# A spectral-filter and GEGLU kernel: another order in its opening, another split of its first weight loads, and its middle spectral stage two places sooner

## The chip, the cores and the metric

The kernel runs on one core of a Trainium2 chip. A core has five engines with instruction streams of their own: TensorE (PE, matrix products, written into PSUM banks), VectorE (DVE), ScalarE (ACT, table functions), GpSimd (POOL) and SyncE (SP, which here only issues DMAs). They wait for each other by semaphores; each works through its own stream in order. DMAs are issued from SP's, ScalarE's and GpSimd's queues. The metric is the device time of one execution in microseconds (us); shorter is better.

## The reference

The input x has 2048 rows of 640 numbers (bf16). What is computed:

```
xn = layernorm(x)                                  # each row: (x - mean) / sqrt(var + 1e-5)
s  = irfft2( rfft2(xn) * (w_r + 1j*w_i) )          # spectral filter over both axes
g  = silu( (gelu(xn @ w_gate) * (xn @ w_up)) @ w_down )   # 640 -> 1536 -> 640
out = x + s * g
```

## The kernel before, in words

Rows are split into 16 slabs of 128 (row index = 16 * partition + slab). `X` holds all of them. Four slabs make a group of 512 columns for the products; `xnT[g]` is the transposed, normalised group.

PE's work is one list, `back`, written out by hand. An item of it is called a place here. A second list, `plan`, says what else is emitted behind each place: `put(s, f, args)` adds a call behind place s. So the order of every engine's stream is the order of emission: first what stands outside the lists, then place 0 and what is put there, place 1, and so on. A tile framework puts in the semaphores; nothing is reordered.

- Before place 0: loads are issued; `warm_pe` runs products on a tile of ones; slab 0 is normalised (`stats`, `root_act`, `norm_parts`) and transposed on PE in two parts (`slab_Tparts`: three blocks and two blocks, through the PSUM pool `psB`, then copied out into `xnT[0]`).
- Places 0 to 15: the first group's products for hidden tiles 0 to 7 (a hidden tile is 128 of the 1536). A hidden tile takes five products with gate weights `Wg` into bank `psg`, evicted by ScalarE with Gelu into `ge` (L837), and five with up weights `Wu` into bank `psu`, evicted by VectorE, which multiplies with `ge` into `UT` (L839). Each of `psg` and `psu` has two buffers, `ge` three. Places 0 and 1 do tiles 0 and 1 for slab 0 and for slab 1 (128 columns each); places 2 to 7 tiles 2 to 7 for both slabs (256 columns); places 8 to 15 tiles 0 to 7 for slabs 2 and 3. In between slabs 1, 2 and 3 are normalised and transposed.
- Places 16 to 35: tiles 8 to 11 at 512 columns, then the down products of group 0. Places 36 to 71, 72 to 107 and 108 to 143: groups 1, 2 and 3. The down products of groups 1 and 2 (places 60 to 71 and 96 to 107) are done by a scheme with seven products in place of eight (`product`, L933).
- The spectral filter runs between these. A forward stage (`slab_S1`, `slab_D`, up to place 56) writes `ZDR` in DRAM; `load_B2` at place 56 reads it back in another order. The middle stage, 12 calls of `s2_step`, starts at place `sb` = 67: PE products `px` from the read-back tile, VectorE products with the filter, PE products `pu`, copies into `RX` and DMAs to `UDR`. `load_V` reads that back, and the inverse stage (`slab_S1i`, `slab_Di`, `group_*`, `finish`) follows at distances counted from `sb`.

A slab's statistics are two `bn_stats` and one `bn_aggr` on VectorE (`bn_half`, `bn_join`). The inverse root comes in two ways: `root_act` (ScalarE's inverse-root table) for slab 0, and `root` (a VectorE add, then a power on GpSimd) for the others. After slab 0's root ScalarE loads the Gelu table. `inv_consts` and `inv_rest` make small constants of the inverse transform on VectorE and GpSimd, at places 0 and 1; `ft_v` (ScalarE) reads them from place 8 on. `tinv_phase` and `ft_phase` (GpSimd) prepare arguments for sine tables; `root` and `shift` of slabs 4 to 7 stand behind them on GpSimd, and `norm_act` of these slabs (ScalarE, from place 15 on) reads what they make.

The lines of the loads, in order of issue on SP: L94 to L106; on ScalarE's queue L231 and L232. `load_w(k, t0, t1)` loads gate (k = 0) or up (k = 1) weights of hidden tiles t0 to t1 - 1: 640 rows of (t1 - t0) * 256 bytes.

Of the kernel before, what the change touches and what calls it, by code (L numbers as in the profile page):

```python
# [14 lines left out]
P = 128  # L15
# [61 lines left out]
def build(nc, env):  # L77
# [8 lines left out]
    def load_w(k, t0, t1, eng=nc.sync):  # L86
        f0, f1 = t0 * P, t1 * P
        eng.dma_start(out=(Wg, Wu)[k][:, :, f0:f1], in_=(wgv, wuv)[k][:, :, f0:f1])

    def load_gu(t0, t1):  # L90
        for k in range(2):
            load_w(k, t0, t1)
# [3 lines left out]
    load_w(1, 0, 2)  # L96
    load_w(1, 2, 4)
    load_x(2, 1)
    load_w(1, 4, 6)
    load_x(3, 1)  # L100
    load_gu(6, 8)
    load_x(4, 4)
    load_gu(8, 12)
    load_x(8, 4)
# [68 lines left out]
    def c1(name, dt=FP32):  # L173
        return consts.tile([P, 1], dt, name=name)
# [27 lines left out]
    def root(n0, n):  # L202
        m = mva[n0 // 4][:, n0 % 4:n0 % 4 + n, :]
        ve = work.tile([P, 4], FP32, tag="ve", name="ve")[:, 0:n]
        nc.vector.tensor_scalar(out=ve, in0=m[:, :, 1], scalar1=1e-5, scalar2=None, op0=ALU.add)  # L205
        r = work.tile([P, 4], FP32, tag="rst", bufs=4, name="rst")[:, 0:n]
        nc.gpsimd.tensor_tensor(out=r, in0=ve, in1=mhalf[:, 0:n], op=ALU.pow)  # L207
        rall[n0] = r
        for k in range(n):
            rstd[n0 + k] = r[:, k:k + 1]  # L210

    def root_act(n1):
        rstd[n1] = c1("rst0")
        nc.scalar.activation(out=rstd[n1], in_=mva[n1 // 4][:, n1 % 4, 1:2], func=ACT.Abs_reciprocal_sqrt, bias=eps)
        nc.scalar.activation(out=warm, in_=negpi, func=ACT.Gelu_apprx_tanh)

    def norm(n1, c0=0, c1_=D):
# [10 lines left out]
    eps = c1("eps")  # L228
    nc.vector.memset(eps, 1e-5)
    nc.scalar.activation(out=warm, in_=eps, func=ACT.Abs_reciprocal_sqrt)  # L230
    for t in (0, 2, 4):  # L231
        load_w(0, t, t + 2, nc.scalar)  # L232
    b_0, b_1 = c1("b_0"), c1("b_1")
    nc.vector.memset(b_0, 320.0)
    nc.vector.memset(b_1, 0.0)
# [348 lines left out]
    def warm_pe(n):  # L584
        if not warm_bank:
            warm_bank.append(bank(0))
        for _ in range(n):
            nc.tensor.matmul(warm_bank[0][:, 0:256], lhsT=ones[:, 0:P], rhs=ones, start=True, stop=True)
# [237 lines left out]
    def ffn_piece(g, t, k, c0, c1_):  # L826
        for j in range(c0 // P, c1_ // P):
            assert ("T", 4 * g + j) in done
        ps = bank(k)[:, c0:c1_]
        WT = (Wg, Wu)[k]  # L830
        for c in range(5):
            nc.tensor.matmul(ps, lhsT=WT[:, c, t * P:(t + 1) * P], rhs=xnT[g][:, c, c0:c1_],  # L832
                             start=(c == 0), stop=(c == 4))
        flush()
        if k == 0:
            ges[t] = work.tile([P, 512], BF16, tag="ge", bufs=3, name="ge")[:, c0:c1_]
            nc.scalar.activation(out=ges[t], in_=ps, func=ACT.Gelu_apprx_tanh)  # L837
        else:
            nc.vector.tensor_tensor(out=UT[:, t, c0:c1_], in0=ps, in1=ges[t], op=ALU.mult)  # L839

    def ffn_part(g, t, h):
        for k in range(2):
            ffn_piece(g, t, k, h * 256, h * 256 + 256)

    def ffn_half(g, t, k):
        ffn_piece(g, t, k, 0, 512)
# [122 lines left out]
            if t == NT - 1:  # L969
                gated(g, j, k, ph)  # L970

    def ffn_slab(j, tk):
        for t, k in tk:
            ffn_piece(0, t, k, j * P, j * P + P)

    GG, UU = ((0, 0), (1, 0)), ((0, 1), (1, 1))

    def run(*items):
        for it in items:
            it[0](*it[1:])  # L980
# [3 lines left out]
    def norm_parts(n1):  # L984
        for a, b in PARTS:
            norm(n1, a * P, b * P)

    def slab_Tparts(n1):
        if n1 == 0:
            xnT[0] = slot(0, 5, 512)  # L990
        for (a, b), ev in zip(PARTS, (nc.vector.tensor_copy, nc.scalar.copy)):
            pt = psB.tile([P, 5, P], BF16, tag="b")
            for c in range(a, b):
                nc.tensor.transpose(out=pt[:, c, :], in_=X[:, n1, c * P:(c + 1) * P], identity=ident)  # L994
            ev(out=xnT[0][:, a:b, n1 * P:n1 * P + P], in_=pt[:, a:b, :])
        done.add(("T", n1))

    NP = 8
    STR = (1, 2)
    back = [(run, (ffn_slab, 0, GG), (norm_parts, 1), (slab_Tparts, 1), (vt_iota, 1), (ffn_slab, 0, UU),  # L1000
             (inv_consts, 0), (inv_consts, 1)),
            (run, (ffn_slab, 1, GG + UU), (stats, 2), (root, 2, 1))]
    for h in range(2):
        for t in range(0 if h else 2, NP):
            back.append((ffn_part, 0, t, h))
        if h == 0:
            back[-1] = (run, (ffn_piece, 0, NP - 1, 0, 0, 256), (slab_Tparts, 3), (ffn_piece, 0, NP - 1, 1, 0, 256))
    for g in range(4):
        for t in range(NP if g == 0 else 0, NT):
            for k in range(2):  # L1010
# [10 lines left out]
    def put(s, *item):  # L1021
        plan[s].append(item)

    put(1, inv_rest)
    put(2, norm, 2)
    put(3, bn_half, 3, 0)
    put(4, bn_half, 3, 1)
    put(4, bn_join, 3)
    put(4, root, 3, 1)
    put(4, slab_T, 2, 1)  # L1030
    put(5, norm, 3)
    for g in range(5):
        put(3 + g, ft_v, g)
        put(8 + g, ft_v, 5 + g)
# [73 lines left out]
    put(z_end, load_B2)  # L1108
    for k in range(2):
        put(TURN + k, mg_turn, k)  # L1110
    sb = 67
    AT = (0, 3, 5, 7, 9, 11, 13, 15, 17, 19, 21)
    for b in range(len(BURSTS)):
        put(sb + AT[b], s2_step, b)
# [18 lines left out]
        for k in range(n):  # L1133
            put(min(d + 8 + k, LAST), finish, n0 + k)

    warm_pe(21)
    bn_half(1, 1)
    bn_join(1)
    root(1, 1)
    norm_parts(0)  # L1140
    slab_Tparts(0)
    warm_pe(2)

    put(5, phase_const)

# [35 lines left out]
```

## Time and profile before

| | us |
|---|---|
| median of 3 runs | 193.73 (193.61 to 193.73) |
| the profiled execution | 193.65 |
| its span | 191.9 |
| PE busy | 186.1 (97%) |
| VectorE busy | 150.9 (79%) |
| ScalarE busy | 131.9 (69%) |
| GpSimd busy | 53.9 (28%) |

The span is what the profiler sees from the first to the last instruction; 1.75 us of the execution lie around it. All times below are us from the span's start. In the profile's lines "PE psg L832" is an operation of line 832 that writes `psg`; "x10" is a count; "[1.54 <-POOL nmr L456]" is idle time of that engine just before, and what ended it. "SPq" and "ACTq" are instructions of the queues that issue DMAs; a row of DMA issues ends with the us from issue to landing.

### The profile page before, as it was taken

The page shows a single profiled execution, that of the slowest core. Times are in us where ns is not written, and L with a number is a line of the kernel's source. Part 1 is how long each engine was busy: PE and PEld are TensorE (multiplying, and loading weights), DVE is VectorE, ACT ScalarE, POOL GpSimd, SP SyncE. Part 2 cuts the span into 40 slices and gives each one's busy share as a digit, 9 for nine tenths or more (in the row PEclk, how much of TensorE's full clock was granted, in tenths as well). Part 3 has the DMA queues.
Part 4 walks back from the last instruction along what each step waited for, and adds up shares of the span by engine and source line. Part 5 has one row for each costly group of instructions (what it writes and reads, how often), then busy time and mean ns, then how long its engine had stood idle before and what let it go on. Part 6 is the DMA issues. An engine that isn't in the chain of part 4 may idle for free.

```text
span 191.9 us, 4068 instructions
## 1 busy us (share of the span) xinstructions
PE 186.1 (97%) x1453; PEld 115.6 (60%) x1469; DVE 150.9 (79%) x364; ACT 131.9 (69%) x241; POOL 53.9 (28%) x91
## 2 busy tenths in 40 slices
PE   7999999999999999999999999999999999999993
PEld 5788854677655665566543334347775555556772
DVE  6787889899799889846978677685445898888973
ACT  4658557957878778536697878634989776876622
POOL 4458768999040200000000000002030134150400
PEclk9999999999999999999999999999999999999999
DMA  6999999948889994249996444149900084778842
GB/s 164 300 329 360 370 332 170 172 99 318 178 165 191 211 300 120 78 111 230 223 108 123 106 103 103 42 107 273 266 5 0 0 117 111 152 153 213 121 174 62
DMA packets 39700, 32.43 MB, mean 169 GB/s; under 512 B 12928, under 2 KB 37760, under 8 KB 39552
## 3 DMA queue, kind: packets, MB, share of 16 engines
q1 hardware_dynamic: 35888, 27.91, 58.6%
q0 software_dynamic: 1824, 3.28, 9.4%
q10 hardware_dynamic: 1968, 0.98, 1.9%
q8 instruction: 11, 0.18, 0.4%
q14 instruction: 9, 0.07, 0.1%
HBM read 19.03 MB, written 7.88 MB: 140 GB/s over the span
## 4 chain that ended last, share of the span: by engine, by line
PE 95%; DMA 2%; DVE 1%; issue 1%; SPq 0%; ACT 0%
PE psu L832 27%; PE psg L832 27%; PE psg L967 7%; PE psg L933 7%; PE psu L967 6%; PE psu L933 5%; PE pu L657 2%; PE pd L762 2%; PE pv L735 2%; PE pz L555 2%; PE pd L573 2%; PE px L628 2%; DMA X<-in_A_x_dram 2%; PE pt L994 1%; PE pd L575 1%
## 5 line engine op out<-in xcount | busy, mean ns | idle before, releaser
L832 PE MATMUL psu<-XG,Wu 128*128 128x512 bf16 (+2 forms) x284 | 60.4, 342 | 0.5 <-issue 0.3
L832 PE MATMUL psg<-XG,Wg 128*128 128x512 bf16 (+2 forms) x280 | 60.1, 341 | 0.6
L839 DVE TENSOR_TENSOR UT<-psu,ge 128x512 bf16<-128x512 f32 (+2 forms) x58 | 34.4, 594 | 13.6 <-PE psu L832 8.1
L837 ACT ACTIVATE ge<-psg 128x512 bf16<-128x512 f32 (+2 forms) x58 | 30.3, 523 | 21.3 <-PE psg L832 20.6
L832 PEld LDWEIGHTS <-Wu 128*128 128x128 bf16 x290 | 25.9, 98 | 20.9 <-issue 3.4
L832 PEld LDWEIGHTS <-Wg 128*128 128x128 bf16 x290 | 26.5, 98 | 18.8 <-issue 0.2
L967 PEld LDWEIGHTS <-UT 128*128 128x128 bf16 x204 | 19.1, 98 | 6.9
L813 POOL DMA_DIRECT2D VY<-in_A_x_dram x12 | 10.6, 964 | 26.2 <-ACT W L737 10.5
L713 POOL COPY vr<-VY 128x128 bf16<-128x128 bf16 x2 | 0.6, 291 | 60.2 <-DMA VY<-UDR 60.2
L644 DVE TENSOR_TENSOR RZ<-xs,W 128x960 bf16<-128x960 bf16 (+2 forms) x22 | 13.3, 647 | 4.4 <-ACT xs L640 4.4
L967 PE MATMUL psg<-Wd,UT 128*128 128x320 bf16 (+1 forms) x108 | 15.7, 290 | 0.0
L578 ACT CAST RZ<-pd 128x660 bf16<-128x660 f32 x16 | 11.3, 706 | 5.2 <-PE pd L575 5.2
L189 DVE BATCH_NORM_STATS2 st<-X 128x6 f32<-128x320 bf16 x32 | 14.0, 476 | 0.6 <-DMA X<-in_A_x_dram 0.4
L933 PEld LDWEIGHTS <-UT 128*128 128x128 bf16 x120 | 11.4, 98 | 4.8 <-issue 0.4
L967 PE MATMUL psu<-Wd,UT 128*128 128x320 bf16 (+1 forms) x96 | 13.9, 293 | 0.0
L737 ACT CAST W<-pv 128x640 bf16<-128x640 f32 x16 | 11.1, 691 | 3.1 <-PE pv L735 3.1
L763 ACT ACTIVATE W<-pd 128x640 bf16<-128x640 f32 x16 | 11.3, 706 | 1.5 <-PE pd L762 1.5
L557 ACT CAST GEN<-pz 128x640 bf16<-128x640 f32 x16 | 11.2, 698 | 1.2 <-PE pz L555 1.2
L672 ACT CAST RX<-pu 128x480 bf16<-128x480 f32 (+3 forms) x22 | 10.8, 489 | 1.1 <-DVE RX L672 0.3
L640 ACT CAST xs<-px 128x960 bf16<-128x960 f32 (+2 forms) x11 | 10.3, 933 | 0.0
L207 POOL TENSOR_TENSOR rst<-ve,mhalf 128x1 f32<-128x1 f32 (+1 forms) x6 | 5.5, 913 | 11.5 <-DVE ve L205 11.5
L933 PE MATMUL psg<-X,UT 128*128 128x320 bf16 x48 | 7.8, 300 | 0.0
(202 smaller groups left out, 302.1 us busy)
## 6 DMA issues: line engine op xcount, KB each, us to landing
ZDR<-RZ SPq DMA_DIRECT2D x16, 160.5 KB, 4.1
UDR<-RX SPq DMA_DIRECT2D x10, 240.8 KB, 3.1
B<-ZDR SPq DMA_DIRECT2D x8, 240.8 KB, 5.2
W<-UDR SPq DMA_DIRECT2D x2, 963.0 KB, 9.1
X<-in_A_x_dram SPq DMA_DIRECT2D x3, 640.0 KB, 10.3
Wd<-in_B_w_down_dram SPq DMA_DIRECT2D x1, 1920.0 KB, 14.6
VY<-in_A_x_dram POOLq DMA_DIRECT2D x12, 160.0 KB, 4.3
out_dram<-VY SPq DMA_DIRECT2D x12, 160.0 KB, 2.8
```

What stands on the lines that cost most here:

```text
L189: nc.vector.bn_stats(out=st_n[n1][:, k, :], in_=X[:, n1, 320 * k:320 * k + 320])
L557: nc.scalar.copy(out=Zt[n1], in_=pz)
L578: nc.scalar.copy(out=zd.rearrange("p c (q e) -> p c q e", e=10), in_=pd[:, :, 0:330].rearrange("p c (e q) -> p c q e", q=33))
L644: nc.vector.tensor_tensor(out=pp[-1], in0=xs, in1=WT[:, :, h0:h0 + n, l0:l0 + w], op=ALU.mult)
L672: copy(out=out, in_=src)
L737: nc.scalar.copy(out=vs, in_=pv)
L763: nc.scalar.activation(out=parts(eobuf, i, 5)[:, :, n1 - DG[i][0], :], in_=pd, func=ACT.Copy, scale=(2.0 if n1 // 4 in BY_SILU else 1.0) / ...
L832: nc.tensor.matmul(ps, lhsT=WT[:, c, t * P:(t + 1) * P], rhs=xnT[g][:, c, c0:c1_], start=(c == 0), stop=(c == 4))
L837: nc.scalar.activation(out=ges[t], in_=ps, func=ACT.Gelu_apprx_tanh)
L839: nc.vector.tensor_tensor(out=UT[:, t, c0:c1_], in0=ps, in1=ges[t], op=ALU.mult)
L933: nc.tensor.matmul(ps, lhsT=lhs[:, t, :], rhs=rhs[:, t, :], start=(t == 0 and i in (0, 1, 3)), stop=(t == 5), skip_group_check=i in (2, 4, ...
L967: nc.tensor.matmul(ph, lhsT=UT[:, t, j * P:(j + 1) * P], rhs=Wd[:, t, c0:c1_], start=(t == 0), stop=(t == NT - 1))
```

## The change

Six things are changed.

- Loads: ScalarE's queue issues one load, gates of tiles 0 to 3, where it issued three (tiles 0 and 1, 2 and 3, 4 and 5). SP loads gates of tiles 4 to 7 in one and up weights of tiles 4 to 7 in one.
- Order ahead of place 0: 19 warming products, then slab 0 is normalised and transposed, then 4 more; only then come the second half of slab 1's statistics and its root, which is now taken on ScalarE; the Gelu table is loaded behind it (`gelu_table`), and slab 1 is normalised.
- Places 0 to 15 are cut in another way, by a new function `ffn_multi`: several hidden tiles side by side in one bank, evicted by one instruction of 512 columns. Places 0 to 3 do tiles 0 to 3 for slab 0 (gates, ups) and for slab 1; places 4 to 7 tiles 4 to 7 for both; places 8 to 15 pairs of tiles for slabs 2 and 3. Slab transposes stand in the middle of places 1, 6 and 7.
- In `slab_Tparts` both parts of slabs 0 and 1 are copied out by VectorE.
- What is put behind places 1 to 5 for slabs 2 and 3 moves; `inv_consts` and `inv_rest` move from places 0 and 1 to place 7, ahead of `tinv_phase`.
- `sb` is 65 in place of 67: the middle stage, and with it all that is counted from it, stands two places sooner.

```diff
--- before.py
+++ after.py
@@ -96,9 +96,9 @@
     load_w(1, 0, 2)
     load_w(1, 2, 4)
     load_x(2, 1)
-    load_w(1, 4, 6)
+    load_w(0, 4, 8)
     load_x(3, 1)
-    load_gu(6, 8)
+    load_w(1, 4, 8)
     load_x(4, 4)
     load_gu(8, 12)
     load_x(8, 4)
@@ -210,8 +210,10 @@
             rstd[n0 + k] = r[:, k:k + 1]
 
     def root_act(n1):
-        rstd[n1] = c1("rst0")
+        rstd[n1] = c1("rst%d" % n1)
         nc.scalar.activation(out=rstd[n1], in_=mva[n1 // 4][:, n1 % 4, 1:2], func=ACT.Abs_reciprocal_sqrt, bias=eps)
+
+    def gelu_table():
         nc.scalar.activation(out=warm, in_=negpi, func=ACT.Gelu_apprx_tanh)
 
     def norm(n1, c0=0, c1_=D):
@@ -228,8 +230,7 @@
     eps = c1("eps")
     nc.vector.memset(eps, 1e-5)
     nc.scalar.activation(out=warm, in_=eps, func=ACT.Abs_reciprocal_sqrt)
-    for t in (0, 2, 4):
-        load_w(0, t, t + 2, nc.scalar)
+    load_w(0, 0, 4, nc.scalar)
     b_0, b_1 = c1("b_0"), c1("b_1")
     nc.vector.memset(b_0, 320.0)
     nc.vector.memset(b_1, 0.0)
@@ -838,9 +839,27 @@
         else:
             nc.vector.tensor_tensor(out=UT[:, t, c0:c1_], in0=ps, in1=ges[t], op=ALU.mult)
 
-    def ffn_part(g, t, h):
-        for k in range(2):
-            ffn_piece(g, t, k, h * 256, h * 256 + 256)
+    def ffn_multi(k, t0, n, c0, c1_, half=None):
+        w = c1_ - c0
+        for j in range(c0 // P, c1_ // P):
+            assert ("T", j) in done
+        if half in (None, 0):
+            cur["m"] = bank(k)[:, 0:n * w].rearrange("p (t w) -> p t w", w=w)
+        ps = cur["m"]
+        WT = (Wg, Wu)[k]
+        for i in range(n) if half is None else range(half * n // 2, (half + 1) * n // 2):
+            for c in range(5):
+                nc.tensor.matmul(ps[:, i, :], lhsT=WT[:, c, (t0 + i) * P:(t0 + i + 1) * P], rhs=xnT[0][:, c, c0:c1_],
+                                 start=(c == 0), stop=(c == 4))
+        if half == 0:
+            return
+        flush()
+        if k == 0:
+            ge = work.tile([P, 512], BF16, tag="ge", bufs=3, name="ge")[:, 0:n * w].rearrange("p (t w) -> p t w", w=w)
+            ges[t0, c0] = ge
+            nc.scalar.activation(out=ge, in_=ps, func=ACT.Gelu_apprx_tanh)
+        else:
+            nc.vector.tensor_tensor(out=UT[:, t0:t0 + n, c0:c1_], in0=ps, in1=ges[t0, c0], op=ALU.mult)
 
     def ffn_half(g, t, k):
         ffn_piece(g, t, k, 0, 512)
@@ -969,12 +988,6 @@
             if t == NT - 1:
                 gated(g, j, k, ph)
 
-    def ffn_slab(j, tk):
-        for t, k in tk:
-            ffn_piece(0, t, k, j * P, j * P + P)
-
-    GG, UU = ((0, 0), (1, 0)), ((0, 1), (1, 1))
-
     def run(*items):
         for it in items:
             it[0](*it[1:])
@@ -988,7 +1001,7 @@
     def slab_Tparts(n1):
         if n1 == 0:
             xnT[0] = slot(0, 5, 512)
-        for (a, b), ev in zip(PARTS, (nc.vector.tensor_copy, nc.scalar.copy)):
+        for (a, b), ev in zip(PARTS, (nc.vector.tensor_copy, nc.scalar.copy if n1 > 1 else nc.vector.tensor_copy)):
             pt = psB.tile([P, 5, P], BF16, tag="b")
             for c in range(a, b):
                 nc.tensor.transpose(out=pt[:, c, :], in_=X[:, n1, c * P:(c + 1) * P], identity=ident)
@@ -997,14 +1010,14 @@
 
     NP = 8
     STR = (1, 2)
-    back = [(run, (ffn_slab, 0, GG), (norm_parts, 1), (slab_Tparts, 1), (vt_iota, 1), (ffn_slab, 0, UU),
-             (inv_consts, 0), (inv_consts, 1)),
-            (run, (ffn_slab, 1, GG + UU), (stats, 2), (root, 2, 1))]
-    for h in range(2):
-        for t in range(0 if h else 2, NP):
-            back.append((ffn_part, 0, t, h))
-        if h == 0:
-            back[-1] = (run, (ffn_piece, 0, NP - 1, 0, 0, 256), (slab_Tparts, 3), (ffn_piece, 0, NP - 1, 1, 0, 256))
+    back = [(run, (ffn_multi, 0, 0, 4, 0, P), (vt_iota, 1)),
+            (run, (ffn_multi, 1, 0, 4, 0, P, 0), (slab_Tparts, 1), (ffn_multi, 1, 0, 4, 0, P, 1)),
+            (run, (ffn_multi, 0, 0, 4, P, 256)),
+            (run, (ffn_multi, 1, 0, 4, P, 256))]
+    for h, k, t0 in ((0, 0, 4), (0, 0, 6), (0, 1, 4), (0, 1, 6)) + tuple((1, k, t) for t in (0, 2, 4, 6) for k in range(2)):
+        back.append((ffn_multi, k, t0, 2, 256 * h, 256 * h + 256))
+    back[6] = (run, (ffn_multi, 1, 4, 2, 0, 256, 0), (slab_T, 2, 1), (ffn_multi, 1, 4, 2, 0, 256, 1))
+    back[7] = (run, (ffn_multi, 1, 6, 2, 0, 256, 0), (slab_Tparts, 3), (ffn_multi, 1, 6, 2, 0, 256, 1))
     for g in range(4):
         for t in range(NP if g == 0 else 0, NT):
             for k in range(2):
@@ -1021,14 +1034,17 @@
     def put(s, *item):
         plan[s].append(item)
 
-    put(1, inv_rest)
-    put(2, norm, 2)
-    put(3, bn_half, 3, 0)
-    put(4, bn_half, 3, 1)
-    put(4, bn_join, 3)
-    put(4, root, 3, 1)
-    put(4, slab_T, 2, 1)
-    put(5, norm, 3)
+    put(1, stats, 2)
+    put(1, root, 2, 1)
+    put(2, bn_half, 3, 0)
+    put(2, bn_half, 3, 1)
+    put(3, norm, 2)
+    put(3, bn_join, 3)
+    put(3, root, 3, 1)
+    put(5, norm_parts, 3)
+    for part in range(2):
+        put(7, inv_consts, part)
+    put(7, inv_rest)
     for g in range(5):
         put(3 + g, ft_v, g)
         put(8 + g, ft_v, 5 + g)
@@ -1108,7 +1124,7 @@
     put(z_end, load_B2)
     for k in range(2):
         put(TURN + k, mg_turn, k)
-    sb = 67
+    sb = 65
     AT = (0, 3, 5, 7, 9, 11, 13, 15, 17, 19, 21)
     for b in range(len(BURSTS)):
         put(sb + AT[b], s2_step, b)
@@ -1133,13 +1149,15 @@
         for k in range(n):
             put(min(d + 8 + k, LAST), finish, n0 + k)
 
-    warm_pe(21)
+    warm_pe(19)
+    norm_parts(0)
+    slab_Tparts(0)
+    warm_pe(4)
     bn_half(1, 1)
     bn_join(1)
-    root(1, 1)
-    norm_parts(0)
-    slab_Tparts(0)
-    warm_pe(2)
+    root_act(1)
+    gelu_table()
+    norm_parts(1)
 
     put(5, phase_const)
```

## The prediction

> **What bounds the kernel now.** I read the page first, then the chain of work that ended last in order of time, then the timeline and the DMA issues of the first 9 us, and at last the timeline of every engine from 11 to 36 us.
>
> ```profile
> span 191.9 us, 4068 instructions
> ...
> POOL 4458768999040200000000000002030134150400
> ...
> PE 95%; DMA 2%; DVE 1%; issue 1%; SPq 0%; ACT 0%
> ```
>
> The last line is the chain, by engine; the one above it is GpSimd (POOL) in 40 slices of 4.8 us, busy tenths. TensorE (PE) is the bound from the first product to the last one. Everything else can only matter by letting PE begin sooner or by making it wait. The chain shows how it begins (start, length, what):
>
> ```profile
> 1.17 3.19 DMA X<-in_A_x_dram
> 4.38 0.90 DVE st L189 x2
> ...
> 5.55 0.15 DVE ve L205
> ...
> 6.05 0.54 PE pt L994 x5
> 6.59 0.22 PE psg L588 x2
> 6.84 0.76 PE psg L832 x10
> 7.60 0.28 PE pt L994 x5
> 7.88 0.56 PE psu L832 x10
> ...
> 9.56 0.55 PE psg L832 x5
> ```
>
> The second slab's load lands at 4.36, its statistics and root run on VectorE, and only then is slab 0 normalised, though slab 0's own root was ready earlier:
>
> ```profile
> 1.18 4.55 PE L588 MATMUL psg<-GEN 128*128 128x256 bf16 x21 [1.18 <-DVE eps L229]
> ...
> 4.29 0.29 ACT L214 ACTIVATE rst<-mva,eps 128x1 f32<-128x1 f32 x1 [2.08 <-DVE mva L195]
> 4.60 1.28 ACT L215 ACT_TABLE_LOAD   x1
> ...
> 5.62 0.63 DVE L218 TENSOR_SCALAR X<-X,mva,rst 128x384 bf16<-128x384 bf16 x2
> ```
>
> **The change, part by part.** Profiled execution: 193.65 us; the median of the runs shown, 193.73, stands 0.08 above it, so I add 0.08 at the end.
>
> *Order on VectorE.* Of what stood before slab 0's normalisation, one statistics half (0.45 of the 0.90 pair) stays; the other half, the join and the root's first step move behind it. Normalisation starts at about 4.38 + 0.45 = 4.85 where it started at 5.62, 0.77 sooner. Transposes and evictions follow by the same distance, so the first product could start at 6.84 - 0.77 = 6.07. Nineteen instead of 21 warming products end at 1.18 + 19 x 0.217 = 5.30, with the transposes due at 5.28. Four instead of two behind them add 2 x 0.11: 6.29. The second eviction of slab 0 and of slab 1 moves from ScalarE to VectorE; VectorE has it done before the fourth product of a piece reads it. This part by itself is worth -0.55.
>
> *Products.* Per column block the same columns are multiplied, but tiles 2 and 3 of slabs 0 and 1 go as 40 products of 128 columns (0.56 for 10) where 20 of 256 stood (0.55 for 5): 2.24 against 2.18, +0.06. Evictions become fewer and wider on engines that PE does not wait for here: nothing.
>
> *Loads.* ScalarE's queue issues one load of 640 KB, gates of tiles 0 to 3, where it issued three of 320 KB; SP issues 14 where it issued 15, with 1 KB rows for tiles 4 to 7. What the first product waits for changes from 320 KB to 640 KB.
>
> ```profile
> 1.19 1.01 ACTq L88 DMA_DIRECT2D Wg<-in_B_w_gate_dram  x2
> 1.64 1.00 SPq L88 DMA_DIRECT2D Wu<-in_B_w_up_dram  x2
> Wg<-in_B_w_gate_dram ACTq DMA_DIRECT2D x1, 320.0 KB, 4.3
> Wu<-in_B_w_up_dram SPq DMA_DIRECT2D x1, 320.0 KB, 5.4
> Wg<-in_B_w_gate_dram ACTq DMA_DIRECT2D x1, 320.0 KB, 6.1
> Wu<-in_B_w_up_dram SPq DMA_DIRECT2D x1, 320.0 KB, 6.7
> 4.00:5.00 1.00, 1.00 (x7) 0.67 (x6) 0.84 (x4) 0.69 (x2) 0.00 (x0) 1.00 1.15 342
> 6.00:9.00 3.00, 2.92 (x45) 2.65 (x46) 2.24 (x13) 1.64 (x6) 1.17 (x2) 1.00 1.15 304
> ```
>
> The last number of an issue row is us from issue to landing, and of a window row GB/s. So the first 320 KB of gates landed at 1.19 + 4.3 = 5.5 and the second at about 1.7 + 6.1 = 7.8; the up weights at 7.05 and at 2.15 + 6.7 = 8.85. How soon 640 KB in one load lands, no row shows. If its second half comes alone, 5.5 + 320/342 = 6.45. If as many bytes of up weights come between, 5.5 + 640/304 = 7.6. I take 6.8: nearer to alone, since the gates' rows become twice as long as those of the up weights, but not alone, since the second half came 2.3 us behind the first before. PE then waits from 6.29 and starts at 6.83: -0.01 in place of -0.55, ends -0.35 and +0.8.
>
> The Trainium skill, "DMA: Bandwidth & Descriptors", section "Queues, rings and completion order", says that each DMA engine goes round robin over the queues it has work for, a packet at a time; with a row as the packet that would put half as many bytes of up weights between, and by it the gates would land at 5.5 + 480/342 = 6.9. The late landing of the second gate load agrees with it.
>
> The second half of the up weights is wanted after 1.12 + 0.56 + 0.28 = 1.96 us of products, so at 8.8, against its 8.85 of before with the same bytes ahead of it. Cost about nothing; but it caps the gain: a start at 6.29 would want it at 8.25.
>
> *Root of slab 1 on ScalarE, its table load behind it.* POOL's power and its vector step go; 0.29 on ScalarE and the 1.28 table load come at about 7.1. The first gate eviction waits for it, until about 9; its bank is wanted again by the fourth gate piece, at 6.83 + 4.76 = 11.6. Slab 1 is normalised by 7.1 + 0.29 + 0.63 = 8.0, its transposes due at 6.83 + 1.68 = 8.5. Covered; without cover the table load would cost up to 1.3.
>
> *Slabs 2 and 3.* Statistics and roots move between the pieces; by the lengths above slab 2 is normalised around 13.4 and its transposes are due at 14.3. Covered.
>
> *The inverse constants go from places 0 and 1 to place 7.* This is the part that I believe costs. POOL works in order, and the place is ahead of Tinv's phase:
>
> ```profile
> 11.84 0.26 POOL L323 TENSOR_SCALAR y_e<-pb,x_e 128x1 f32<-128x1 f32 x1
> ...
> 13.57 0.26 POOL L323 TENSOR_SCALAR k_m<-pb,y_m 128x1 f32<-128x1 f32 x1
> 15.50 2.38 POOL L334 TENSOR_SCALAR GEN<-GEN,u,ph_t 128x1024 int32<-128x1024 int32 x2 [0.67 <-DVE ph_t L282]
> 21.21 1.49 POOL L374 TENSOR_TENSOR GEN<-GEN 128x660 f32<-128x660 f32 x1
> 25.27 1.04 POOL L207 TENSOR_TENSOR rst<-ve,mhalf 128x4 f32<-128x4 f32 x1 [2.57 <-DVE ve L205]
> 26.58 0.20 POOL L456 TENSOR_TENSOR nmr<-nm,rst 128x4 f32<-128x4 f32 x1
> 26.81 0.92 ACT L461 ACTIVATE X<-X,nmr,rst 128x640 bf16<-128x640 bf16 x1 [1.54 <-POOL nmr L456]
> 27.64 0.58 ACT L837 ACTIVATE ge<-psg 128x512 bf16<-128x512 f32 x1
> 28.24 0.69 DVE L839 TENSOR_TENSOR UT<-psu,ge 128x512 bf16<-128x512 f32 x1 [0.62 <-ACT ge L837]
> 30.88 0.64 DVE L839 TENSOR_TENSOR UT<-psu,ge 128x512 bf16<-128x512 f32 x1
> 29.55 1.24 PE L832 MATMUL psg<-XG,Wg 128*128 128x512 bf16 x5
> 32.79 1.24 PE L832 MATMUL psu<-XG,Wu 128*128 128x512 bf16 x5
> ```
>
> Place 7 ends on PE 1.12 + 1.40 + 1.12 + 1.12 + 1.09 + 1.09 + 1.37 + 1.37 = 9.68 us after the start, at 16.5; its multiplication on VectorE ends near 17.4, the constants follow, and POOL's six steps (11.84 to 13.83 before) run from 17.55 to 19.5. Tinv's phase starts at 19.5 in place of 15.5. From there to the end of the third FT step POOL needs 22.70 - 15.50 = 7.2: it is free at 26.7, where the root of slabs 4 to 7 began at 25.27 after 2.57 idle. So the idle time takes most of the delay and 1.43 is left. ScalarE already waits 1.54 for nmr; it now gets it at 28.2, and its eviction of the ninth tile's gates (27.64 + 0.58) ends at 29.65. PE wants that bank at 29.55: 0.1. VectorE's multiplication behind it comes 1.45 later, the next one ends near 33.0 behind two statistics, and PE wants its bank at 32.79 + 0.1: 0.15. Together +0.27; ends 0 (if POOL's steps run shorter) and 0.7 (half of the 1.43, if VectorE's and ScalarE's lateness reaches the folds behind).
>
> *Middle stage at place 65 in place of 67* (place k is the k-th piece of PE's work). Steps, the loads that read them back and the inverse stage all come two places sooner, the distances stay. What is new is how near the first step comes to its read of ZDR:
>
> ```profile
> 82.94 6.26 SPq L603 DMA_DIRECT2D B<-ZDR  x10
> B<-ZDR SPq DMA_DIRECT2D x1, 240.8 KB, 4.1
> 88.04 1.63 PE psg L933 x12
> 89.67 0.32 PE px L628 x2
> ```
>
> The first step needs the first two of ten loads; the second is issued at about 83.55 and lands 4.1 later, at 87.65. Two products sooner than 89.67 (1.63) is 88.04. It fits by 0.4. The transposes on SP and the UDR writes keep their order. The end hangs on the last products, not on this stage. Zero; if the load were 1 us late, +0.6.
>
> *Sum:* -0.01 + 0.06 + 0.27 + 0 = +0.32; 193.65 + 0.32 + 0.08 = 194.05.
>
> **Rivals.**
> 1. *The loads come early and POOL's lateness is absorbed.* For it: the window rate of 342 before the short rows begin. Gates at 6.45, start 6.5, -0.34 + 0.06: 193.45. Against it: the cap of the up weights. To be faster by more than 0.39 it needs a start under 6.4 and no wait later: 193.3.
> 2. *The gates land late (slower).* The two queues share by bytes: 7.6, start 7.65, +0.81 + 0.06 + 0.27: 194.85. It decides from a landing of 6.9 on, with the POOL wait. For it: 2.3 us between the two gate loads of before. Against it: the short rows of the up weights.
> 3. *POOL's lateness reaches further.* The start as forecast, but the bank waits sum to 0.7: 194.5. For it: in its slices POOL stands at 8 and 9 tenths from 29 to 48 us, so nothing is made up there. Against it: from 48 us on it is idle, and most of what it makes is used later.
> 4. *PE's clock rises later.* The 21 warming products took 0.217 each, the two behind the transposes 0.11. With 19 and a pause the rise could miss its time; every us at half speed costs 0.5, so 195 with 2 us more. Against it: a pause of 0.3 stood there before too. The Trainium skill, "TensorE: Matmul & The Clock Gate", section "Part 1", has the gate open after a window of about 3.4 us of activity, and 19 products are 4.1 us; by that rule it opens in time.
> 5. *The reorder does nothing*, start and waits cancelling: 193.75.
>
> **How the numbers follow.** Forecast (193.9 to 194.2) 0.32; rival 1 0.17, of it 0.09 under 193.34; rival 5 0.13; rival 2 0.18; rival 3 0.15; rival 4 0.05. About 0.2% (0.39) is what can be told from no change: 193.34 to 194.12 holds two thirds of the forecast (0.21), 0.08 of rival 1 and rival 5, so 0.43 with rounding; slower is the rest of the forecast, 2, 3 and 4: 0.48; faster 0.09. The range goes from rival 1, 193.5, to rival 2, 194.85; the likeliest alone has 193.9 to 194.2.
>
> **What would show it.** Transposes of slab 0 near 5.3; a wait of PE before the first product released by the load of Wg, 0.3 to 0.8; Tinv's phase at 19.5; ScalarE's wait for nmr about 3 us; short waits of PE for banks at 29 to 33 us; px near 88 without a wait. Wrong would make it: a first product under 6.4 or over 7.2, or PE without any pause between 25 and 36.

## The result and the profile after

| | before | after |
|---|---|---|
| median of 16 executions each, same chip | 193.82 us | 194.77 us |
| ratio after/before, 95% interval | | 1.0053 (1.0038 to 1.0068) |
| the profiled execution | 193.65 | 194.63 |
| its span | 191.9 | 192.6 |
| time outside the span, mean | 1.78 (of the executions beside the experiments) | 1.98 |

One of the 16 executions before took 327.87 us; the ratio is taken without it. The change costs about 0.95 us. The forecast was +0.32, so the sign and the range held and the size did not. The profiled pair differs by 0.98, and its traces show where it went. First the page of the changed kernel: GpSimd's slices and the chain by engine.

```profile
span 192.6 us, 4074 instructions
...
POOL 4323999899240200000000000002110506224000
...
PE 86%; POOL 6%; DMA 3%; issue 1%; DVE 1%; SPq 1%; ACT 0%; ACTq 0%; DVEq 0%
```

GpSimd, which was on no stretch of the chain before (PE had 95%), now carries 6% of it. The chain in order of time shows it, in two windows (start, length, what):

```profile
2.10 6.13 DMA Wu<-in_B_w_up_dram
...
8.28 0.73 PE psu L852 x10
```

```profile
15.63 0.56 PE psu L852 x5
16.28 0.69 DVE UT L862
...
19.18 2.39 POOL GEN L335 x2
...
22.37 2.99 POOL GEN L373
...
25.43 1.81 POOL GEN L375
...
28.51 0.21 POOL nmr L457
...
29.57 0.58 ACT ge L838
30.20 1.24 PE psg L833 x5
```

The opening now hangs on the second load of up weights, not on the gates. From place 7 the chain goes over VectorE's multiplication, all of GpSimd's work on Tinv and FT (the tables that `tinv_phase` and `ft_phase` prepare; L335, L373 and L375), the root of slabs 4 to 7 with their shift `nmr`, and ScalarE's Gelu, and comes back to PE at 30.20. The row of the gates' load among the DMA issues, and the timelines of PE, GpSimd, ScalarE and VectorE at the same places:

```profile
Wg<-in_B_w_gate_dram ACTq DMA_DIRECT2D x1, 640.0 KB, 4.8
```

```profile
5.20 0.54 PE L1007 MATMUL pt<-ident,X 128*128 128x128 bf16 x5
5.58 0.60 PE L589 MATMUL psg<-GEN 128*128 128x256 bf16 x4
6.08 1.31 PE L852 MATMUL psg<-XG,Wg 128*128 128x128 bf16 x20
...
24.74 1.24 PE L833 MATMUL psg<-XG,Wg 128*128 128x512 bf16 x4
...
27.98 1.24 PE L833 MATMUL psu<-XG,Wu 128*128 128x512 bf16 x5
30.20 1.24 PE L833 MATMUL psg<-XG,Wg 128*128 128x512 bf16 x5 [0.97 <-ACT ge L838]
...
34.59 1.66 PE L986 MATMUL psg<-Wd,UT 128*128 128x320 bf16 x11
...
188.47 0.83 PE L986 MATMUL psg<-Wd,UT 128*128 128x128 bf16 x12
```

```profile
22.37 2.98 POOL L373 TENSOR_SCALAR GEN<-GEN 128x660 f32<-128x660 f32 x1
...
28.74 0.92 ACT L462 ACTIVATE X<-X,nmr,rst 128x640 bf16<-128x640 bf16 x1 [4.29 <-POOL nmr L457]
...
22.29 0.76 DVE L340 TENSOR_SCALAR GEN<-GEN,andm,orm 128x1024 int32<-128x1024 int32 x1
...
24.72 0.65 DVE L205 TENSOR_SCALAR ve<-mva 128x4 f32<-128x4 f32 x1
```

The matching rows of before: the first of GpSimd's two FT steps, place 16 (at 25.24), the first down products and the last products.

```profile
18.68 2.45 POOL L372 TENSOR_SCALAR GEN<-GEN 128x660 f32<-128x660 f32 x1
...
25.24 1.24 PE L832 MATMUL psg<-XG,Wg 128*128 128x512 bf16 x4
...
33.87 1.79 PE L967 MATMUL psg<-Wd,UT 128*128 128x320 bf16 x12
...
187.82 0.83 PE L967 MATMUL psg<-Wd,UT 128*128 128x128 bf16 x12
```

Read by stages, after minus before:
- First product 6.08 against 6.84: -0.76. At place 16 it is 24.74 against 25.24: -0.50. Of the gain, 0.23 went into the wait for the up weights at 8.28, and 0.06 into the 128-column products.
- From place 16 to the first down product 9.85 (34.59 - 24.74) against 8.63 (33.87 - 25.24): +1.22. It is the wait of 0.97 and what is lost around it.
- From there to the last products 153.88 against 153.95: -0.07.
- From the last products to the end of the span (the traces have it to hundredths) 192.65 - 188.47 = 4.18 against 191.87 - 187.82 = 4.05: +0.13. Part 6 shows what stands there.
- The time outside the span is 194.63 - 192.65 = 1.98 against 193.65 - 191.87 = 1.78: +0.20.

-0.50 + 1.22 - 0.07 + 0.13 + 0.20 = +0.98.

### The profile page after: what moved, and what is told of

Read it like the earlier page. It is cut to its first block, busy times and chain, and to the rows that moved or that the text cites. A ratio compares the mean times of both kernels' runs of the same rounds, so it can differ in the third digit from the quotient of the medians.

```text
span 192.6 us, 4074 instructions
## 1 busy us (share of the span) xinstructions
PE 186.0 (97%) x1473; PEld 116.1 (60%) x1489; DVE 151.2 (78%) x358; ACT 130.3 (68%) x230; POOL 53.4 (28%) x90
## 4 chain that ended last, share of the span: by engine, by line
PE 86%; POOL 6%; DMA 3%; issue 1%; DVE 1%; SPq 1%; ACT 0%; ACTq 0%; DVEq 0%
PE psu L833 21%; PE psg L833 21%; PE psg L986 7%; PE psg L952 7%; PE psu L986 6%; PE psu L952 5%; DMA Wu<-in_B_w_up_dram 3%; PE pu L658 2%; PE pv L736 2%; PE pd L763 2%; PE pz L556 2%; PE psu L852 2%; PE pd L574 2%; PE px L629 2%; PE psg L852 2%; POOL GEN L373 2%
## 5 line engine op out<-in xcount | busy, mean ns | idle before, releaser
L833 PE MATMUL psg<-XG,Wg 128*128 128x512 bf16 x190 | 48.7, 379 | 1.5 <-ACT ge L838 1.0
L833 PE MATMUL psu<-XG,Wu 128*128 128x512 bf16 x194 | 49.0, 379 | 0.5 <-issue 0.3
L840 DVE TENSOR_TENSOR UT<-psu,ge 128x512 bf16<-128x512 f32 x40 | 27.4, 687 | 12.4 <-PE psu L833 6.8
L838 ACT ACTIVATE ge<-psg 128x512 bf16<-128x512 f32 x40 | 23.9, 598 | 15.4 <-PE psg L833 14.5
L833 PEld LDWEIGHTS <-Wu 128*128 128x128 bf16 x200 | 18.0, 98 | 20.3 <-issue 3.4
L833 PEld LDWEIGHTS <-Wg 128*128 128x128 bf16 x200 | 18.6, 98 | 19.2 <-issue 1.3
L852 PE MATMUL psu<-XG,Wu 128*128 128x256 bf16 (+1 forms) x100 | 10.4, 251 | 0.1
L852 PE MATMUL psg<-XG,Wg 128*128 128x256 bf16 (+1 forms) x100 | 10.0, 251 | 0.0
```

Of the source, the lines that this page charges most:

```text
L852: nc.tensor.matmul(ps[:, i, :], lhsT=WT[:, c, (t0 + i) * P:(t0 + i + 1) * P], rhs=xnT[0][:, c, c0:c1_], start=(c == 0), stop=(c == 4))
```

## The experiments

Theory A: GpSimd's order costs the time. The constants behind place 7 delay Tinv, FT, the root and so the Gelu whose bank PE wants. Theory F, formed when the first four runs came back with unequal times outside the span: the ends of the instruction streams cost too. Rivals stand with each run. The kernel before ran beside each group: 193.72 us (first four runs), 193.57 (next four), 193.56 and 193.57.

### 1. The constants alone, taken out and put in

Inverse constants back to the middle of place 1 in the changed kernel:

```
-             (run, (ffn_multi, 1, 0, 4, 0, P, 0), (slab_Tparts, 1), (ffn_multi, 1, 0, 4, 0, P, 1)),
+             (run, (ffn_multi, 1, 0, 4, 0, P, 0), (slab_Tparts, 1), (inv_consts, 0), (inv_consts, 1), (inv_rest,),
+              (ffn_multi, 1, 0, 4, 0, P, 1)),
...
-    for part in range(2):
-        put(7, inv_consts, part)
-    put(7, inv_rest)
```

> The changed kernel with one thing undone: the inverse constants (five steps on VectorE, six on GpSimd) stand in the middle of place 1 again, ahead of Tinv's phase, instead of at place 7. Theory A (GpSimd's order costs the time): Tinv's phase starts near 14.6 instead of 19.2, the last FT step ends near 22 instead of 27.2, nmr is there near 26.3, TensorE's one wait of 1.0 us for the Gelu eviction (ended 30.20) is gone, and the time falls by 0.9 to 1.1 to 193.6 to 193.9; against the kernel before the ratio is 0.998 to 1.000. Rival B (the loss lies in the new cut of places 0 to 15, in its 512-column evictions and its bank order): the wait stays in another form and the time falls by less than 0.3, to 194.5 or more.

Measured: 194.29 us, ratio 1.003 (1.0013 to 1.0046), profiled span 191.9. Of the three rows below the first is GpSimd's, the second VectorE's and the third PE's; no wait is left near 30.

```profile
14.79 2.38 POOL L335 TENSOR_SCALAR GEN<-GEN,u,ph_t 128x1024 int32<-128x1024 int32 x2 [0.85 <-DVE ph_t L283]
...
15.44 0.69 DVE L862 TENSOR_TENSOR UT<-psu,ge 128x512 bf16<-128x512 f32 x1 [0.76 <-ACT XG L548]
...
16.45 1.25 PE L852 MATMUL psg<-XG,Wg 128*128 128x256 bf16 x10 [0.16 <-DVE XG L1008]
```

A holds for the wait: from place 16 to the first down product it is 33.81 - 25.18 = 8.63 again, to the hundredth what the kernel before takes. In the whole only half of the loss came back (0.5% to 0.3%, with intervals that overlap), less than expected. Two things took the rest. Place 8 began at 16.45 instead of 16.01: 0.1 of it came from the opening, and 0.3 because VectorE's multiplication of place 6, due at about 15.0, began at 15.44, with GpSimd's Tinv phase running beside it since 14.79. (The row names ScalarE's copy L548 as what ended the wait; in the changed kernel the same multiplication began at 14.91, before that copy had ended, so it doesn't hang on it.) And this execution took 2.17 outside its span; the twelve had 1.8 to 3.4.

The same part alone in the kernel before (constants out of place 0, `put(7, inv_consts, ...)`, `put(7, inv_rest)`):

> The kernel before with this one part of the change alone: inverse constants at place 7. Theory A: GpSimd's six steps run near 17.4 to 19.4, Tinv's phase starts there, the FT steps end near 26.7 to 27.4, nmr comes at 28.0 to 28.7, and TensorE waits 0.2 to 0.8 for the Gelu eviction of the ninth tile, near 29.6 to 30.2; less than in the changed kernel, since TensorE reaches that place 0.5 later here. Time 194.0 to 194.6, ratio 1.001 to 1.004. The prediction's term for it was 0.27, with ends 0 and 0.7. Rival B: no wait, ratio 0.999 to 1.001.

Measured: 194.36 us, ratio 1.0029 (1.0015 to 1.0044), 1.79 outside the span. GpSimd, VectorE and PE:

```profile
24.95 1.50 POOL L374 TENSOR_TENSOR GEN<-GEN 128x660 f32<-128x660 f32 x1
...
25.12 1.36 DVE L205 TENSOR_SCALAR ve<-mva 128x4 f32<-128x4 f32 x1
...
26.86 1.24 PE L832 MATMUL psu<-XG,Wu 128*128 128x512 bf16 x5 [0.52 <-DVE UT L839]
```

The part costs 0.64 by itself (from place 16 to the first down product 34.41 - 25.09 = 9.32, +0.69), but in another place than expected: not over `nmr` and the Gelu. VectorE's step `ve` on four columns (0.17 in the kernel before) took 1.36: it ended at 26.48, with GpSimd's step at 26.45. The multiplication queued behind it came late, and PE waited for its bank. The Trainium skill, "SBUF — State Buffer", section "SBUF: two separate sides", calls the port pair that VectorE and GpSimd share an exclusive lock: a GpSimd instruction or a VectorE instruction of certain forms, whichever starts first, gets it for the whole instruction, and the other is blocked. These two rows agree; rows of parts 2 and 5 do not.

### 2. Why GpSimd's two FT steps were longer

`put(14, tinv_mask, 1)` becomes `put(19, tinv_mask, 1)`:

> The changed kernel with VectorE's second mask step of Tinv (128x1024 int32) at place 19 instead of 14, so that it doesn't run beside GpSimd's FT steps. Theory C (the two FT steps of 2.98 and 1.81, which took 2.45 and 1.49 before, are held up by VectorE's mask and root step beside them): they go back to about 2.45 and 1.49, nmr comes 0.7 to 0.85 sooner, near 27.9, TensorE's wait falls from 0.97 to 0.1 to 0.4, time 193.9 to 194.2. Rival D (they are longer for another cause, the loads or ScalarE's work beside them): their lengths stay, the wait stays near 1.0, time 194.6 to 194.9.

Measured: 195.19 us (194.63 to 195.77, 6 executions), ratio 1.0076 (1.0053 to 1.0099), profiled span 192.6. GpSimd, then VectorE, then the waits of PE:

```profile
22.39 2.45 POOL L373 TENSOR_SCALAR GEN<-GEN 128x660 f32<-128x660 f32 x1
24.93 1.49 POOL L375 TENSOR_TENSOR GEN<-GEN 128x660 f32<-128x660 f32 x1
...
22.35 1.34 DVE L340 TENSOR_SCALAR GEN<-GEN,andm,orm 128x1024 int32<-128x1024 int32 x1
```

```profile
PE psg L986 <- DVE UT L840: 0.3, 1, 0.3
PE psg L833 <- ACT ge L838: 0.2, 1, 0.2
```

The steps went back to 2.45 and 1.49 and the wait near 30 to 0.24, as C says. The edit explains only the second step. Beside the first one VectorE's first mask, not moved, took 1.34 in place of 0.76: this time VectorE lost. In both traces the mask had begun first, by 0.08 in the changed kernel and by 0.04 here; in the traces of parts 3 and 4 that have the same pair it began 0.05 ahead, and GpSimd lost (3.00). So C holds, the two engines delay each other, but what decides who loses stays open. The mask ended at 23.69 while GpSimd's step ran on to 24.84, so it was held for only a part of that step. The time did not fall. The moved mask ran at 32.70, the multiplications behind it came no sooner than in the changed kernel (34.65 against 34.61), and PE waited at 36.0: the first down products began 0.68 sooner than in the changed kernel (33.91 against 34.59), the second ones only 0.07 (36.15 against 36.22). Why the executions of this run spread over 1.1 us stays open.

### 3. The loads of the opening

The changed kernel with the gates of tiles 0 to 3 in two loads:

```
-    load_w(0, 0, 4, nc.scalar)
+    load_w(0, 0, 2, nc.scalar)
+    load_w(0, 2, 4, nc.scalar)
```

> The changed kernel with the gates of the first four tiles as two loads of 320 KB (rows of 512 bytes, as in the kernel before) on ScalarE's queue in place of one of 640 KB. Theory H (the gates come early because their rows are 1 KB against 512 bytes of the up weights in the other queue, so the queues share in proportion to the row): the second gate load lands at 7.0 to 7.8 instead of 6.0, TensorE stops 0.3 to 1.0 in the middle of place 0, and the second up load lands sooner than 8.2, at about 7.5. Rival I (the 640 KB came early because one issue was saved on the queue): it lands within 0.3 of 6.0 and nothing else moves. The end comes by the wait of 1.0 near 30 either way, up to 0.4 later by theory H.

Measured: 195.51 us, ratio 1.0088 (1.0064 to 1.0113), profiled span 193.5. PE's waits:

```profile
PE psg L853 <- DMA Wg<-in_B_w_gate_dram: 1.2, 1, 1.2
PE psg L834 <- ACT ge L839: 1.0, 1, 1.0
```

H holds in its direction: with rows of 512 bytes the second half came at 7.8 (PE began with it at 7.87), with rows of 1 KB all of it at 6.0. The second up load did not come sooner, as H had it, but later (6.6 us to land against 6.1). The second row shows that PE came to place 20 about 1 us later and still waited 1.0: GpSimd's chain starts from place 7 and so moves with PE. A late opening doesn't hide it.

### 4. The ends of the instruction streams

The changed kernel with 13 one-column memsets on VectorE and 12 one-column copies on ScalarE added:

```
+    for k in range(13):
+        put(104 + 2 * k, pad_v)
+    for k in range(12):
+        put(13 if k < 4 else 14, pad_s)
```

> The changed kernel with 13 more one-column memsets on VectorE (late, from place 104 on) and 12 more one-column copies on ScalarE (places 13 and 14, where it stood idle), which compute nothing that is used. Theory F (the change took 13 recorded instructions from VectorE and 19 from ScalarE, and so the last fetch of an 8 KB block of code of each engine, which before ran at 176.4 and 186.6 inside the span, now falls at 194.0 and 194.4, behind its end, and lengthens the execution there): both fetches move back inside the span, none is left behind 192.6, the time outside the span falls from 1.9 to 2.0 to 1.75, and the execution gets 0.2 to 0.3 shorter, 194.4 to 194.6. Rival G (the fetches are idle reading and cost nothing): the time outside the span stays at 1.9 to 2.0 and the time at 194.7 to 194.9, or more by the added work.

Measured: 194.49 us, ratio 1.0045 (1.003 to 1.0059); 1.85 outside the span on the mean (median 1.81). The DMA view of 193 to 195 us, behind the span's end, of the changed kernel and of this one:

```profile
DMA packets 2, 0.02 MB, mean 8 GB/s; under 512 B 0, under 2 KB 0, under 8 KB 0
...
q14 instruction: 2, 0.02, 2.3%
```

```profile
DMA packets 0, 0.00 MB, mean 0 GB/s; under 512 B 0, under 2 KB 0, under 8 KB 0
```

F holds for the fetches and for the time outside the span, 0.13 less on the mean. The gain in the whole (1.0053 to 1.0045) has its sign, but the intervals overlap. With fewer instructions on VectorE and ScalarE the fetch of the last 8 KB of code of each fell behind the program's work. In the traces the time outside the span goes with it: 1.78 to 1.79 in six without such a fetch, 1.98 to 2.18 in five with two. But it isn't the only cause: the two traces of the kernel with place 67 in part 6 have 2.05 and 1.91 and no fetch behind the end.

The middle stage back at place 67 in the changed kernel (`sb = 67`):

> The changed kernel with the middle stage back at place 67. All theories but one: within 0.1 us of the changed kernel, since px did not wait there; the wait at 30.20 stays at 1.0 and px starts about 1.6 later. Rival E (the middle stage two places sooner costs or wins time at its end): the time moves by 0.3 or more.

Measured: 195.71 us, ratio 1.0102 (1.0081 to 1.0122). The profiled span is 192.7, as in the changed kernel, but 2.56 us lie outside it on the mean and 3.57 in the profiled execution. The same view from 193 to 197 us:

```profile
q8 instruction: 1, 0.02, 2.5%
```

A 16 KB fetch now stands there as well, taken for one of PE's code (this queue fetches 16 KB each 11 to 22 us through the kernel, one fetch for 250 to 270 of PE's recorded instructions). On PE's own path the "within 0.1" held: from place 16 to the last products 188.47 - 24.67 = 163.80 against 163.73. The loss in the whole lies mostly outside the span, by a mechanism that none of the theories had.

### 5. A version that keeps the gain

Constants ahead of place 0, where VectorE waits for ScalarE's root and GpSimd is idle:

```
     root_act(1)
     gelu_table()
+    inv_consts(0)
+    inv_consts(1)
+    inv_rest()
```

> The changed kernel with the inverse constants ahead of place 0, between the join of slab 1's statistics and its normalisation, where VectorE waits 0.37 for ScalarE's root and GpSimd is idle. Theory A: Tinv's phase starts near 14.6, nmr is there by 26.9, no wait near 30, and, other than with the constants in the middle of place 1, nothing in the opening comes later: place 16 starts at 24.7 to 24.9 against 25.24 in the kernel before, the down products at 33.3 to 33.5 against 33.87. Span 0.3 to 0.5 shorter than before; with a time outside the span of 1.9 to 2.2 the execution comes to 193.4 to 193.8. Rival: the gain of the opening isn't kept, time 194.0 to 194.4.

Measured: 193.97 us, ratio 1.0017 (0.9999 to 1.0036), profiled span 191.8, no wait near 30; but place 8 at 16.43 and place 16 at 25.16, as with the constants in place 1. The rival had it: the gain of the opening isn't kept.

With the small instructions of part 4 added:

> Both: constants ahead of place 0 and the added small instructions on VectorE and ScalarE. Theories A and F together: no wait near 30, no code fetch behind the span's end, 1.75 outside the span, time 193.2 to 193.5, faster than the kernel before by 0.2 to 0.5 (ratio 0.9975 to 0.999). If F is wrong: as the kernel without the added instructions, 193.4 to 193.8.

Measured: 193.73 us, ratio 1.0011 (0.9992 to 1.0031), 1.80 outside the span on the mean against 1.98: the same sign again, 0.24 less with 25 more instructions, within the intervals. It is no faster than the kernel before.

With `phase_const` put behind place 7 instead of place 5, so that Tinv's phase doesn't start beside place 6's multiplication:

> Constants ahead of place 0 and the added small instructions, and one thing more: the one-column VectorE step that makes ph_t, on which GpSimd's Tinv phase waits, stands behind place 7 instead of place 5, so that the phase (1.2 us a step) does not start at 14.79 beside VectorE's multiplication of place 6. Theory J (that multiplication began 0.41 late, at 15.42 to 15.48 in three runs against 14.91 in the changed kernel, because GpSimd's step had begun at 14.79; the copy of slab 3 behind it came later by as much, and place 8 with it): Tinv's phase starts near 17.0, the multiplication at 14.9 to 15.1, place 8 at 16.0 to 16.1 instead of 16.43 to 16.49, place 16 at 24.7 to 24.9, no wait near 30 (FT steps end near 24.2, nmr 26.3 to 26.6), down products at 33.35 to 33.5, span 191.3 to 191.6, time 193.1 to 193.4, ratio 0.997 to 0.999. Rival K (the delay has another cause): place 8 stays at 16.4, time 193.6 to 193.9.

Measured: **193.25 us**, ratio to the kernel before 0.9987 (0.9974 to 0.9999), where the changed kernel had 1.0053. PE and GpSimd:

```profile
16.01 1.25 PE L852 MATMUL psg<-XG,Wg 128*128 128x256 bf16 x10
...
24.75 1.24 PE L833 MATMUL psg<-XG,Wg 128*128 128x512 bf16 x4
...
17.15 2.39 POOL L335 TENSOR_SCALAR GEN<-GEN,u,ph_t 128x1024 int32<-128x1024 int32 x2 [3.22 <-DVE ph_t L283]
```

Theory J holds: place 8 is at 16.01 again, though the phase now runs later. The multiplication of place 6 began at 14.91, the down products at 33.38. What holds VectorE back for 0.41 in the first part of GpSimd's step, and not for the whole of it, stays open; the lock as the Trainium skill tells it would have held it to 15.98. This kernel is faster than the changed one by 0.66% and than the kernel before by 0.13%, with an interval just clear of 1. Its step from the version ahead of it (1.0011 to 0.9987) has the expected sign, but those two intervals still overlap.

### 6. What the two places are worth

The fastest kernel with the middle stage at place 67, twice:

> The same with the middle stage back at place 67, so that the two stand side by side without a code fetch behind the end. If the place of the middle stage is worth nothing, as the prediction's term for it says: equal within 0.15, 1.75 to 1.85 outside the span. If the 0.9 that the changed kernel lost with place 67 came from the stage itself and not from the code fetches behind the end: 0.5 to 0.9 slower.

> A second look at the fastest kernel with the middle stage at place 67, to see which of the two waits of its first profile belong to that place: the 0.75 for the gate load in the opening should be gone or small if it was the chance of one execution, and the wait of 0.5 for the read-back should be there again, 0 to 0.6, with less than 0.5 between GpSimd's copies and the product. Time 193.4 to 194.5 against 193.25 for place 65.

Measured: 194.4 us (ratio 1.0045, 1.0026 to 1.0064) and 194.65 (1.005, 1.003 to 1.0071), so by the ratios 1.1 and 1.2 us more than at place 65. PE's waits of the first and of the second, and GpSimd's copy and PE's product of the first:

```profile
PE psg L852 <- DMA Wg<-in_B_w_gate_dram: 0.8, 1, 0.8
PE pv L736 <- POOL vr L716: 0.5, 1, 0.5
```

```profile
PE psg L852 <- DVE x_w L273: 0.4, 1, 0.4
PE pv L736 <- POOL vr L716: 0.3, 1, 0.3
```

```profile
133.50 0.28 POOL L716 COPY vr<-VY 128x128 bf16<-128x128 bf16 x1
...
133.84 0.23 PE L736 MATMUL pv<-Tinv,vr 128*128 128x128 bf16 x1 [0.47 <-POOL vr L716]
```

With this earlier opening and place 67 PE waits for the read-back of the middle stage. In the kernel before the same copy ended about 0.4 ahead of its product; at place 65 it is more:

```profile
132.66 0.29 POOL L715 COPY vr<-VY 128x128 bf16<-128x128 bf16 x1
...
133.35 0.22 PE L735 MATMUL pv<-Tinv,vr 128*128 128x128 bf16 x1
```

```profile
130.84 0.36 POOL L716 COPY vr<-VY 128x128 bf16<-128x128 bf16 x1
...
132.37 0.22 PE L736 MATMUL pv<-Tinv,vr 128*128 128x128 bf16 x1
```

These are the kernel before and the changed one: 133.35 - 132.95 = 0.4 and 132.37 - 131.20 = 1.2. The two places are a cover. The other wait, for the gate load, is in both traces of this kernel (the load took 5.4 and 6.0 us to land; the second row names VectorE's `x_w`, long done, but 1.19 + 6.0 is 7.2, when PE began). The eight other traces with this load have 4.6 to 4.9. Nothing links it to the middle stage. From place 16 to the last products these two traces took 163.2 and 163.1 us, against 162.5 at place 65: 0.6 to 0.7 lies behind the opening, and the waits show 0.3 to 0.5 of it. The opening took 0.3 and 0.9 more, and the time outside the span, expected at 1.75 to 1.85, was 2.01 and 2.15 on the mean against 1.86. So the 1.1 to 1.2 isn't all the stage's.

The stage at place 65 alone in the kernel before:

> The kernel before with the middle stage at place 65 alone. Theory L (at place 67 the read-back of the middle stage's result comes only 0.4 ahead of the products that need it, and late executions wait there; two places sooner make it 1.2 or more): as the kernel before or slightly faster, ratio 0.997 to 1.000, GpSimd's copies of the read-back end 1.2 or more ahead of the product that reads them, and the slower executions get rarer. If the stage's place is worth 0.9 to 1.1 by itself, as the two pairs of the changed kernels had it: 192.5 to 192.9. If it is worth nothing, as the prediction's term says: within 0.1.

Measured: 193.91 us, ratio 1.0018 (1.0008 to 1.0029): none of the three expectations holds. The copy comes 0.7 ahead of its product (130.99 against 131.66), not 1.2, PE's last products come as early as before (187.76 against 187.82), and yet the span ends 0.3 later, at 192.2. In the trace's semaphore records, SP ends the program by waiting for its DMAs' semaphores in a fixed order, 0.06 apart. In the kernel before the last output's semaphore is the last of them. Here it is the second of nine, and the seven behind it take 0.43 more. The loss is at the program's end, not in the stage. In the changed kernel it is the seventh of nine, and the two behind it take 0.12: that is the +0.13 of its last 4 us, since the last output lands 3.05 us behind the first of the last products in both kernels.

## Why the prediction was right, and where not

- **Direction and range: right, with the mechanism named.** It gave 0.48 to slower, put the cost into the constants at place 7, and drew its path: GpSimd, nmr, ScalarE's eviction, PE's bank. The trace has this path, and moving the constants away removes the wait. That the total fell into the range is luck in part: its upper end, 194.85, was worked out from gates that land late, and they landed early.
- **"Together +0.27": mis-sized.** It measured +1.22, beyond its upper end of 0.7 (0.64 alone in the kernel before). The path's pieces: Tinv's phase at 19.18 (forecast 19.5); from there to nmr 9.5 us (28.72) against 8.7, since the two FT steps took 0.85 longer; then 1.43 through ScalarE, 1.45 in the forecast. And PE wanted the bank at 29.06, not 29.55: a place 0.5 sooner is a wait 0.5 longer where the other end is fixed by GpSimd. The step took the durations of GpSimd's instructions as fixed, when they depend on what VectorE starts beside them. Rival 3 came nearest (waits of 0.7), with a chance of 0.15.
- **"Worth -0.55" for the order on VectorE: more, -0.76 at the first product.** The transposes came at 5.20, near the forecast 5.28. The sum charged 0.22 for the two more warming products behind them; these ran from 5.58, while the copies into `xnT` were made, and the first product still began at 6.08.
- **"I take 6.8" for the gates: wrong, below both ends.** They landed at 1.19 + 4.8 (the row of the DMA issues after) = 6.0. Both ends set out from the first half's landing at 5.5. As one load with rows of 1 KB the first half must have been in by about 5.0 (an estimate: the second half at the 332 GB/s that moved from 5 to 6 us takes 1.0); as a load of its own with rows of 512 bytes it came at 5.3 in part 3. The Trainium skill's turn by packets gave 6.9, with a row taken as the packet; its direction agrees with the split loads, its time does not. In two traces of ten it was 6.6 and 7.2, on both sides of the value taken.
- **Second up weights, "caps the gain": right.** 0.23 of wait at 8.28 against a want at 8.04.
- **Products +0.06, slabs 2 and 3, root of slab 1: right.** 40 products took 11.09 - 8.85 = 2.24, and no wait stands there.
- **Middle stage "zero": right in this change** (-0.07, px at 88.69 without a wait), but short of what it does: it takes the read-back from 0.4 to 1.2 of slack, and without it the earlier PE of part 6 waits 0.3 to 0.5.
- **Clock: rival 4 is real, and small.** In the changed kernel the granted clock rose at 5.39, and the four products behind the transposes took 0.60. In the version of part 1 it rose at 6.29, they took 0.87, and the first product came at 6.45. That 19 products open the clock in time doesn't hold in general: in six of the fourteen traces it rose only at 5.99 to 7.16.
- **Missing from the sum:** the end. +0.20 of the 0.98 lies outside the span and +0.13 in the wait for the DMAs' semaphores; every line of the sum had counted both as nothing. Added instructions took 0.13 of the first back, on the mean.

Of the signs named: transposes near 5.3 (5.20), Tinv at 19.5 (19.18), px near 88 without a wait (88.69) held. PE's wait for the gate load did not come; ScalarE waited 4.29 for nmr instead of about 3; and in place of short waits there was one of 0.97. A first product under 6.4 was named as what would make the prediction wrong; it came, and with that the sum would have been about 193.5, faster. Two errors of opposite sign, -0.55 in the opening and +0.95 at the bank, and the terms left out, +0.33 together, made the forecast look better than its steps.

## What to carry to other kernels

When a step is emitted later in an engine's stream, follow that engine in order to the next instruction that another engine waits for, and size each piece with what will run beside it. A wait that hangs on the place it is put at moves with the stream, so an earlier start doesn't pay for it: put preparation where its engine is idle and nothing else is timed by it. And compare the last 4 us and the time outside the span of both kernels: here they moved by 0.13 and 0.20, with other numbers of instructions and another order of semaphores.

## What the runs showed of the hardware that was not expected

- VectorE and GpSimd delay each other for parts of a step: GpSimd's FT step took 2.45 or 2.98, VectorE's mask 0.76 or 1.34, a four-column add 0.17, 0.65 or 1.36. With the mask 0.04 to 0.08 ahead GpSimd lost four times and VectorE once.
- Code is fetched by DMA while the kernel runs, 16 KB at a time on one queue (taken for PE's) and 8 KB on another (VectorE's and ScalarE's moved when instructions were added there). A fetch behind the end goes with a longer execution: 1.78 us outside the span without one, 1.98 with two of 8 KB, 3.57 in an execution with one of 16 KB as well. With 25 instructions added the mean came back to 1.80 and 1.85. Two traces with 1.91 and 2.05 have no such fetch.
- The end of the program depends on the place of the last DMA's semaphore in SP's order: 0.43 us for seven behind it, 0.12 for two, none where it was the last.
- One load of 640 KB with rows of 1 KB landed in 4.6 to 4.9 us in eight of ten traces (5.4 and 6.0 in the others) beside a queue with rows of 512 bytes; as two loads with rows of 512 bytes its second half came 1.8 us later.
- The granted clock rose to full between 3.83 and 7.16 us in fourteen traces, with warming products from 1.18 on in all of them.
